# Placing one accumulator at the right end of SBUF and one constant among the experts' tiles, so that every large tile begins at a multiple of 512 bytes

## The chip, the cores and the metric

One Trainium2 chip, one of its cores. The metric is the device time of one launch in microseconds (us), lower being better. The kernel before takes 572.62 us, the median of three runs (572.4 to 574.07).

## What is computed

Three stages in float32, the output of one being the input of the next: causal linear attention with a decay per head, a dense layer pair with a squared ReLU, and a layer pair with eight experts, of which each token uses one.

```python
# attention: q, k, v are (2, 8, 768, 64), in blocks of 64
intra = (qb @ kb.T * Dmask) @ vb
inter = (qb * lam_pow) @ kv_state
kv_state = lam_block * kv_state + (kb * rev_pow).T @ vb
x = out.transpose(0, 2, 1, 3).reshape(1536, 512)
# dense layer pair: w_in is (512, 2048), w_out (2048, 512)
h = np.maximum(x @ w_in, 0.0)
x = h * h @ w_out
# experts: w1 is (8, 512, 1024), w2 (8, 1024, 512)
e_idx = np.argmax(x @ w_gate, axis=1)
out[mask] = gate_w * eom * (np.maximum(x[mask] @ w1[e], 0.0) @ w2[e])
```

## The kernel before

Products that need more than one pass of rounding are made of three: each operand is split into a rounded high part and a remainder (names ending in h and l), and high times high, high times low and low times high are added up in PSUM. A split is a copy on ScalarE (ACT) that writes the high part and a subtraction on VectorE (DVE) or GpSimd (POOL) that writes the low part.

**Attention** runs over 12 units (batch, 128 rows). SP loads q, k and v four units ahead, in order, mixed with raw pieces `st` of w_in and w_out. TensorE (PE) transposes q and k (L257, L259), makes the scores (L287), the output (L301, L305) and the state (L331).

**The dense pair** goes over three chunks of 512 tokens (`ch`) and, in each, over 16 blocks of 128 hidden columns (`f`): 48 steps `s`. In step s, PE makes the hidden block with 12 matmuls of 512 columns (`mm1`, L360; weights `wih`, `wil`; moving data `xTh`, `xTl`) and adds the block of two steps earlier to four output accumulators with 12 more (`mm2`, L488; weights `woh`, `wol`; moving data `gh`, `gl`). Between them `act1` makes gh and gl: ACT the ReLU `r` (L367) and, in the first chunk, the square `g` (L370), then gh (L377); DVE gl (L378). In the first chunk ACT and DVE also turn the loaded weights from 64-bit to 32-bit floats (L130 on ACT; L131, L134 and L138 on DVE, two pieces a step), and the order of both engines' work is that of the text. Between the blocks of chunks 1 and 2 stand the routing of the chunk before (L519 to L701), some 20 short PE jobs.

**The experts**: `emm1` (L925) makes eight hidden blocks with 12 matmuls each, 192, 256 or 384 tokens wide by the expert's count, `emm2` (L947) the output of up to three groups of 128 tokens, 24 matmuls of 512 columns a group. The weights of w1 (L801, L802) are split into the space that xTh and xTl leave. Groups j = 1 and 2 stand behind a branch, with nothing else for PE between their matmuls.

**Where tiles lie.** SBUF is handed out by pools as stacks, from the left end up or, with `side="right"`, from the right end down. `const` (small tables, the accumulator `sacc` of 480 bytes and the constant `over` of 32 among them) comes first on the left, then xTh and xTl, the raw weight buffers `w1`, `w2` of even experts, and the stage's pools. The right side holds q and k during attention (pool ldqk), and after it the split weights wih, wil, woh and wol (pool sp); the first gathered rows `xg0` reuse wih and wil. The experts' own pools (ep, xe, ec) come after the dense pair's are given back; ec holds the raw weights of odd experts.

In a matmul, `lhsT` is what PE loads as weights (LDWEIGHTS, shown as PEld) and `rhs` what it streams:

```python
nc.tensor.matmul(out=ps, lhsT=w_[:, kk, :], rhs=x_[:, kk, tk], ...)          # L360: wih, wil | xTh, xTl
nc.tensor.matmul(out=acc[ch][cb], lhsT=w_[:, cs], rhs=x_, ...)               # L488: woh, wol | gh, gl
nc.tensor.matmul(out=ea[j], lhsT=h_[:, f, js], rhs=w_, ...)                  # L947: hh, hl | w2h, w2l
```

Every such weight block is 128 floats, 512 bytes of each partition, and follows the one before it without a gap.

Of the kernel before, what the change touches and what calls it, by code (L numbers as in the profile page):

```python
# [9 lines left out]
F32 = mybir.dt.float32  # L10
# [14 lines left out]
def attn_moe_kernel(ctx, tc, q, k, v, lam, w_in, w_out, w_gate, w_ogate, w1, w2, out):  # L25
# [4 lines left out]
    E, _, F2 = w1.shape  # L30
    P = 128
# [9 lines left out]
    NG = NSL + 1  # L41
    NW = 5

    ctx.enter_context(tc.manual_schedule())
    const = ctx.enter_context(tc.tile_pool(name="const", bufs=1))
# [20 lines left out]
    wg = const.tile([P, KC, 32], F32, name="wg")  # L66
    nc.gpsimd.memset(wg, 0.0)
    cnti = const.tile([P, E], I32, name="cnti")
    over = const.tile([P, E], F32, name="over")
    overi = const.tile([P, 1], I32, name="overi")  # L70
    caps = const.tile([P, E], F32, name="caps")
    nc.gpsimd.memset(caps, float(NG * P))
# [3 lines left out]
    nc.gpsimd.memset(csum, 0.0)  # L76
    sidx = const.tile([P, NG, E], I32, name="sidx")
    gidx = const.tile([P, NG, E], I32, name="gidx")
    sacc = const.tile([P, NG, NW, E], F32, name="sacc")
    gate = const.tile([P, NG, E], F32, name="gate")  # L80
    pp1 = const.tile([P, 1], F32, name="pp1")
    nc.gpsimd.iota(pp1, [[0, 1]], base=1, channel_multiplier=1, allow_small_or_imprecise_dtypes=True)
# [539 lines left out]
    def route_poh(ch, j):  # L622
        pos, pay = rps[ch]
        poh = (xe[0] or gp[0]).tile([P, NTT, P], BF16, tag="poh", name="poh", bufs=3 if xe[0] else 2)
        for t in range(NTT):
            nc.vector.tensor_scalar(out=poh[:, t, :], in0=slots[:, j * P:(j + 1) * P], scalar1=pos[:, t, :],
                                    scalar2=None, op0=ALU.is_equal)
        rhs_[ch, j] = poh
# [45 lines left out]
    def route_slot(ch, j):  # L674
        slot_mm(ch, [j])
        slot_fin(ch, [j])
# [105 lines left out]
    def w2_of(e, f):  # L782
        return w2r[(e * NF2 + f) // (NF2 // 2)][:, f % (NF2 // 2), :]

    side = {1: [route_base, route_logits], 2: [route_max], 3: [route_rank, route_sum, route_pay], 4: [route_gate, route_gate1, route_gate2],
            5: [lambda c: route_poh(c, 0)], 6: [lambda c: route_slot(c, 0), lambda c: route_poh(c, 1)],
            7: [lambda c: route_slot(c, 1), lambda c: route_poh(c, 2)], 8: [lambda c: route_slot(c, 2)]}
# [75 lines left out]
    ep = ctx.enter_context(tc.tile_pool(name="ep", bufs=1, reuse_waits="tile"))  # L863
# [13 lines left out]
    xg = [ep.tile([P, DM], F32, tag=f"xg{j}", name="xg") for j in range(NG)]  # L877
    ys = [ep.tile([P, DM], F32, tag=f"y{j}", name="y") for j in range(NG)]

    tt = ep.tile([P, 2], I32, name="tt")  # L880
    ti = ep.tile([P, 1], I32, name="ti")

    def gather(out_, ix):
# [212 lines left out]
```

## Time and profile before

| | |
|---|---|
| time, median of 3 runs | 572.62 us |
| profiled execution, its own time | 572.36 us |
| its span | 570.6 us |
| PE busy in the span | 549.9 us (96%) |
| DVE / ACT / POOL busy | 361.4 (63%) / 304.3 (53%) / 148.5 (26%) |
| clock granted to PE | 1.00 in every slice but the last |

The span is one execution seen by the hardware profiler. The stages lie at about 0 to 68 us (attention), 63 to 344 us (the dense pair) and 344 to 562 us (experts). "Busy" of PE counts a matmul from its start to the modelled end of its last column, and neighbours overlap: the time that a matmul costs a stream of matmuls is the distance between two starts, not its duration. Rows that name several forms average over them.

### The profile page before, as it was taken

What the parts mean: (1) busy time and instruction counts of PE and PEld (TensorE: products, weight loads), DVE (VectorE), ACT (ScalarE), POOL (GpSimd) and SP (SyncE); (2) the same over time, 40 slices, a digit from 0 to 9 for tenths busy, and PEclk for the clock granted to TensorE, in tenths of its full rate; (3) what the DMA queues carried; (4) which work ended last, traced back from release to release, by engine and by line L of the source; (5) the groups of instructions that cost most, each with busy time, mean ns of one, the idle gap of its engine ahead of it and who ended that gap; (6) DMA issues with size and microseconds to landing.
All of it is one profiled execution on the core that took longest, in us unless ns stands there. A gap on an engine that the chain in (4) does not pass through costs nothing. (4 is left out here: it accounts for less than half of the span.)

```text
span 570.6 us, 9451 instructions
## 1 busy us (share of the span) xinstructions
PE 549.9 (96%) x3418; PEld 461.9 (81%) x3418; DVE 361.4 (63%) x728; ACT 304.3 (53%) x580; POOL 148.5 (26%) x149
## 2 busy tenths in 40 slices
PE   8998899999999999999999999899999999999994
PEld 7787788888877877887877888789887988888893
DVE  5679988898455664547676446948264839776510
ACT  4766477776543444445454434536364847885610
POOL 4788000000021222422123240350303042240101
PEclk9999999999999999999999999999999999999998
DMA  9999345459000010000000003999638567740000
GB/s 190 234 266 247 124 143 213 167 202 344 25 0 2 20 37 20 0 1 0 20 20 19 20 0 134 382 250 302 199 121 277 183 212 243 262 153 21 10 22 24
DMA packets 75044, 72.87 MB, mean 128 GB/s; under 512 B 30181, under 2 KB 61029, under 8 KB 74976
## 3 DMA queue, kind: packets, MB, share of 16 engines
q1 hardware_dynamic: 70624, 62.96, 36.4%
q0 software_dynamic: 4064, 8.91, 5.0%
q8 instruction: 42, 0.69, 0.5%
q14 instruction: 26, 0.21, 0.1%
q10 hardware_dynamic: 288, 0.10, 0.1%
HBM read 65.84 MB, written 9.29 MB: 132 GB/s over the span
## 5 line engine op out<-in xcount | busy, mean ns | idle before, releaser
L348 POOL TENSOR_TENSOR wol<-woF,woh 128x512 fp32r<-128x512 f32 x32 | 41.6, 1300 | 228.1 <-ACT woh L347 228.1
L378 DVE TENSOR_TENSOR gl<-g,gh 128x512 fp32r<-128x512 f32 x48 | 52.9, 1103 | 67.8 <-ACT gh L377 67.8
L925 PE MATMUL ph<-xh,xTh 128*128 128x192 f32 (+2 forms) x256 | 77.4, 303 | 6.4 <-PEq L1060 2.7
L940 DVE SCALAR_TENSOR_TENSOR hl<-ph,hh 128x384 fp32r<-128x384 f32 (+1 forms) x64 | 34.5, 539 | 68.2 <-ACT hh L939 68.2
L360 PE MATMUL ps<-xTh,wih 128*128 128x512 f32 x192 | 77.5, 404 | 0.0
L488 PE MATMUL acc<-gh,woh 128*128 128x512 f32 x192 | 76.1, 396 | 0.3 <-DVE x1T L500 0.2
L488 PE MATMUL acc<-gl,woh 128*128 128x512 f32 x192 | 75.8, 395 | 0.0
L360 PE MATMUL ps<-xTl,wih 128*128 128x512 f32 x192 | 75.8, 395 | 0.0
L360 PE MATMUL ps<-xTh,wil 128*128 128x512 f32 x192 | 75.8, 395 | 0.0
L488 PE MATMUL acc<-gh,wol 128*128 128x512 f32 x192 | 75.8, 395 | 0.0
L925 PE MATMUL ph<-xh,xTl 128*128 128x192 f32 (+2 forms) x256 | 74.6, 292 | 0.0
L925 PE MATMUL ph<-xl,xTh 128*128 128x192 f32 (+2 forms) x256 | 74.3, 292 | 0.0
L347 ACT CAST woh<-woF 128x512 fp32r<-128x512 f32 x48 | 29.6, 616 | 60.3 <-PE acc L488 60.2
L925 PEld LDWEIGHTS ph<-xh,xTh 128*128 128x128 f32 x256 | 48.6, 190 | 15.0 <-DVE hl L940 7.3
L939 ACT ACTIVATE hh<-ph 128x384 fp32r<-128x384 f32 (+1 forms) x64 | 30.7, 480 | 41.0 <-PE ph L925 37.9
L367 ACT ACTIVATE r<-ps 128x512 f32<-128x512 f32 x48 | 28.6, 595 | 39.1 <-PE ps L360 39.1
L925 PEld LDWEIGHTS ph<-xl,xTh 128*128 128x128 f32 x256 | 48.6, 190 | 0.7
L925 PEld LDWEIGHTS ph<-xh,xTl 128*128 128x128 f32 x256 | 48.8, 191 | 0.0
L884 POOL DMA_INDIRECT xg<-x1d,gidx x21 | 23.4, 1116 | 88.9 <-PE pt L904 66.0
L802 DVE TENSOR_TENSOR xTl<-w1r,xTh 128x512 fp32r<-128x512 f32 x64 | 44.1, 690 | 0.1
L488 PEld LDWEIGHTS acc<-gh,woh 128*128 128x128 f32 x192 | 36.0, 187 | 9.9 <-DVE x1T L500 1.2
L952 POOL DMA_INDIRECT out_dram<-y,sidx x23 | 23.6, 1027 | 76.4 <-ACT y L951 67.9
(185 smaller groups left out, 1160.1 us busy)
## 6 DMA issues: line engine op xcount, KB each, us to landing
w1r<-in_moe_w_dram SPq DMA_DIRECT2D x32, 512.0 KB, 6.5
w2r<-in_moe_w_dram SPq DMA_DIRECT2D x32, 512.0 KB, 7.1
st<-in_moe_w_in_dram SPq DMA_DIRECT2D x16, 512.0 KB, 3.8
st<-in_moe_w_out_dram SPq DMA_DIRECT2D x16, 512.0 KB, 4.4
q<-in_q_dram SPq DMA_DIRECT2D x24, 128.0 KB, 4.4
k<-in_k_dram SPq DMA_DIRECT2D x12, 256.0 KB, 4.6
v<-in_v_dram SPq DMA_DIRECT2D x12, 256.0 KB, 5.0
x1d<-xr SPq DMA_DIRECT2D x12, 256.0 KB, 2.0
```

What stands on the lines that cost most here:

```text
L347: nc.scalar.copy(out=hi, in_=src)
L348: eng.tensor_tensor(out=lo, in0=src, in1=hi.bitcast(F32), op=ALU.subtract)
L360: nc.tensor.matmul(out=ps, lhsT=w_[:, kk, :], rhs=x_[:, kk, tk], start=n == 0, stop=n == 3 * KC - 1)
L367: nc.scalar.activation(out=r, in_=ps, func=AF.Relu)
L378: nc.vector.tensor_tensor(out=gl, in0=g, in1=gh.bitcast(F32), op=ALU.subtract)
L488: nc.tensor.matmul(out=acc[ch][cb], lhsT=w_[:, cs], rhs=x_, start=f == 0 and i == 0, stop=f == NF - 1 and i == 2)
L802: eng.tensor_tensor(out=lo, in0=src, in1=hi.bitcast(F32), op=ALU.subtract)
L884: nc.gpsimd.indirect_dma_start(out=out_, out_offset=None, in_=x1d[:, :], in_offset=bass.IndirectOffsetOnAxis(ap=ix, axis=0), bounds_check= ...
L925: nc.tensor.matmul(out=ps[:, 0:N], lhsT=w_[:, kk, :], rhs=x_[:, kk, 0:N], start=n == 0, stop=n == 3 * KC - 1)
L939: nc.scalar.activation(out=hh[:, f, ts_], in_=ps[:, ts_], func=AF.Relu)
L940: nc.vector.scalar_tensor_tensor(out=hl[:, f, ts_], in0=ps[:, ts_], scalar=0.0, in1=hh[:, f, ts_].bitcast(F32), op0=ALU.max, op1=ALU.subtract)
L952: nc.gpsimd.indirect_dma_start(out=outs[j][:, :], out_offset=bass.IndirectOffsetOnAxis(ap=sidx[:, j, e:e + 1], axis=0), in_=ys[j], in_offs ...
```

## The change

The accumulator `sacc` leaves `const` for a pool of its own at the right end. The constant `over` leaves `const` for the experts' pool ep, and a pad of 224 bytes is put there behind the small tile `tt`. Nothing else is edited.

```diff
@@ -66,7 +66,6 @@
     cnti = const.tile([P, E], I32, name="cnti")
-    over = const.tile([P, E], F32, name="over")
     overi = const.tile([P, 1], I32, name="overi")
@@ -76,7 +75,9 @@
     gidx = const.tile([P, NG, E], I32, name="gidx")
-    sacc = const.tile([P, NG, NW, E], F32, name="sacc")
+
+    rend = ctx.enter_context(tc.tile_pool(name="rend", bufs=1, side="right"))
+    sacc = rend.tile([P, NG, NW, E], F32, name="sacc")
     gate = const.tile([P, NG, E], F32, name="gate")
@@ -877,7 +878,9 @@
+    over = ep.tile([P, E], F32, name="over")
     tt = ep.tile([P, 2], I32, name="tt")
+    ep.tile([P, 56], F32, name="pad")
     ti = ep.tile([P, 1], I32, name="ti")
```

The instructions of both programs, their order on each of the five engines and the semaphores that they wait for are the same, row for row. What differs are the addresses. Byte offsets in a partition (the first buffer of each name), and what is left of them when divided by 512:

| tiles | before | mod 512 | after | mod 512 |
|---|---|---|---|---|
| xTh, xTl | 21504, 46080 | 0 | 20992, 45568 | 0 |
| raw w1, w2 of even experts | 70656, 87040 | 0 | 70144, 86528 | 0 |
| hh, hl, w2h, w2l, xh, xl, xg, y | 136192 (hh) | 0 | 135680 (hh) | 0 |
| st, r, g, gh, gl, v, kd, sm, qd | 189440 (gh) | 0 | 188928 (gh) | 0 |
| raw w1, w2 of odd experts | 177920, 194304 | 256 | 177664, 194048 | 0 |
| q, wih, wil (right side) | 212960 (wih) | 480 | 212480 (wih) | 0 |
| k, woh, wol (right side) | 221152 (woh) | 480 | 220672 (woh) | 0 |
| sacc | 19808 | 352 | 228864 | 0 |
| over | 18976 | 32 | 172544 | 0 |

So the two groups whose place within 512 bytes changes and that are large are the right side (480 to 0) and the odd experts' raw weights (256 to 0). Everything on the left moves down by 512 bytes together. Small tiles (sidx, gidx, lgT, poh and others) move too, by 32 to 512 bytes.

## Rows read from the trace of the kernel before

**Rows 1.** Busy us, dense pair: PE, PEld, DVE, ACT, POOL; PEclk, DMA share, GB/s

```profile
75.00:340.00 265.00, 264.72 (x1250) 211.08 (x1249) 168.63 (x333) 135.31 (x243) 51.49 (x40) 1.00 0.18 64
```

**Rows 2.** Groups by form, two of the matmuls (busy us, mean ns, idle before)

```profile
L360 PE MATMUL ps<-xTh,wil 128*128 128x512 f32 x192 | 75.8, 395 | 0.0
...
L947 PE MATMUL ea<-xTl,hh 128*128 128x512 f32 x102 | 40.0, 392 | 0.0
```

**Rows 3.** Timeline of PE, dense pair, first matmuls of blocks (start, us, what)

```profile
94.27 0.40 PE L360 MATMUL ps<-xTh,wih 128*128 128x512 f32 x1
...
97.07 0.40 PE L488 MATMUL acc<-gh,woh 128*128 128x512 f32 x1
...
99.87 0.40 PE L360 MATMUL ps<-xTh,wih 128*128 128x512 f32 x1
```

**Rows 4.** Timeline of PE, experts 0 and 1, groups of L947

```profile
376.15 0.48 PE L947 MATMUL ea<-xTh,hh 128*128 128x512 f32 x1
...
378.30 0.39 PE L947 MATMUL ea<-xTh,hh 128*128 128x512 f32 x1
...
381.70 0.33 PE L925 MATMUL ph<-xh,xTh 128*128 128x384 f32 x1
...
405.37 0.39 PE L947 MATMUL ea<-w2h,hh 128*128 128x512 f32 x1
...
410.81 0.39 PE L947 MATMUL ea<-w2h,hh 128*128 128x512 f32 x1
```

**Rows 5.** Timeline of PE, dense pair, a block behind a routing job

```profile
273.92 0.48 PE L360 MATMUL ps<-xTh,wih 128*128 128x512 f32 x1
...
276.79 0.40 PE L488 MATMUL acc<-gh,woh 128*128 128x512 f32 x1
```

**Rows 6.** Timelines of DVE and PE while DVE rests

```profile
342.66 0.69 DVE L500 COPY x1T<-acc 128x512 f32<-128x512 f32 x1 [1.75 <-PE acc L488]
...
341.06 0.40 PE L488 MATMUL acc<-gh,woh 128*128 128x512 f32 x1
...
342.46 0.40 PE L488 MATMUL acc<-gh,woh 128*128 128x512 f32 x1
```

**Rows 7.** Groups by form, weight loads of L360 and of two transposes

```profile
L360 PEld LDWEIGHTS ps<-xTh,wil 128*128 128x128 f32 x192 | 36.0, 188 | 8.9
...
L904 PEld LDWEIGHTS pt<-ident,xg 128*128 128x128 f32 x56 | 6.9, 140 | 1.8
...
L259 PEld LDWEIGHTS psk<-ident,k 128*128 128x128 f32 x48 | 5.5, 141 | 0.8 <-DMA k<-in_k_dram 0.6 <-ACT ca L268 0.2
```

**Rows 8.** Timeline of PE, expert 6: three matmuls of L947 between L925

```profile
494.56 0.42 PE L947 MATMUL ea<-xTh,hh 128*128 128x512 f32 x1
...
495.28 0.25 PE L925 MATMUL ph<-xh,xTh 128*128 128x192 f32 x1
```

**Rows 9.** Timelines of DVE (steps 1 and 11) and PE (step 1), first chunk

```profile
78.81 0.69 DVE L378 TENSOR_TENSOR gl<-g,gh 128x512 fp32r<-128x512 f32 x1
...
134.54 0.69 DVE L378 TENSOR_TENSOR gl<-g,gh 128x512 fp32r<-128x512 f32 x1
...
80.51 0.39 PE L488 MATMUL acc<-gl,woh 128*128 128x512 f32 x1
```

**Rows 10.** Waits of weight loads, 150 to 344 us (us in total, times, longest)

```profile
PEld acc L488 <- DVE x1T L500: 1.2, 2, 0.6
```

**Rows 11.** DMA issues (count, size, median us to landing)

```profile
k<-in_k_dram SPq DMA_DIRECT2D x12, 256.0 KB, 4.6
v<-in_v_dram SPq DMA_DIRECT2D x12, 256.0 KB, 5.0
```

**Rows 12.** Splits on ACT by form, and the reads of raw w1 (min/median/max ns)

```profile
L377 ACT CAST gh<-g 128x512 fp32r<-128x512 f32 x48 | 29.6, 617 | 5.4 <-DVE g L372 5.4
L347 ACT CAST woh<-woF 128x512 fp32r<-128x512 f32 x48 | 29.6, 616 | 60.3 <-PE acc L488 60.2
...
L801 ACT CAST xTh<-w1r x64: 607/612/632, 258.0 to 539.1; 128x512 fp32r<-128x512 f32 x64
```

## The prediction

> **What bounds the kernel now.** First I read the busy time by stretches. From 75 to 340 us, the dense pair, PE is busy 264.72 of 265 us at a granted clock of 1.00, DVE 168.63, ACT 135.31, and the DMA share is 0.18 [rows 1]. So this half of the span is as long as PE's matmuls take, and nothing but the distance from one matmul's start to the next can shorten it. Durations don't tell that distance: they are 395 ns for a dense matmul and 392 for an expert one, both 512 columns wide [rows 2]. The timeline does. In the dense pair the first matmuls of three blocks stand at 94.27, 97.07 and 99.87 us: 12 matmuls in 2.80 us, 233.3 ns each, in mm1 and mm2 alike [rows 3]. In the experts, 24 matmuls of the same width follow each other from 405.37 to 410.81 us: 5.44 us, 226.7 ns each [rows 4]. At the 2.4 GHz of a granted 1.00 these are 560 and 544 cycles. The same instruction costs 6.7 ns more in the dense pair, and there are 48 x 24 = 1152 of them: up to 7.7 us.
>
> What makes the difference? Not other engines: before 342.66 us DVE has rested for 1.75 us, and inside that rest six matmuls take from 341.06 to 342.46, 233 ns each [rows 6]. Not the moving tensor or the PSUM bank: mm1 (xTh, one bank for 12) and mm2 (gh and gl, a new bank after every three) run at the same 2.80 [rows 3]. Not a passing disturbance either: after the restart at 376.15 an expert group is at its pace by 378.30 (from there 15 matmuls in 3.40 us, to 381.70 [rows 4]), while the dense blocks never reach it. What mm1 and mm2 share and L947 hasn't is the place of the weights: wih to wol begin 480 bytes past a multiple of 512, hh and hl at a multiple. That is inference from one kernel; no row shows an off-place tile moved.
>
> **The change, part by part.** It removes and adds no instruction, and moves none. It changes places.
>
> *Right side, weights of mm1 and mm2 (480 to 0).* If the place is the cause, a step of 24 matmuls goes from 5.60 to 5.44 us, 0.16 less. Three things take some of 48 x 0.16 = 7.7 back.
> First, the first chunk has a second clock. DVE's gl of step 1 starts at 78.81, that of step 11 at 134.54: 5.573 us a step [rows 9]. In the text's order DVE waits for ACT's woh and ACT's g for DVE's last gl; the two pace each other, slightly faster than PE's 5.600, so they don't follow PE now and won't speed up with it. At step 1 gl ends at 78.81 + 0.69 = 79.50 and is used at 80.51 [rows 9]: 1.01 us to spare. Ten steps on it is 10 x 0.027 more, 1.28. PE gains 0.16 a step until that slack is used, about step 7, and then runs at 5.573, some 0.13 us of waiting a step. By step 12, the last with conversions ahead of its gl, it is ahead by the slack there, 1.2 with some semaphore time off, not 13 x 0.16 = 2.1. The other 35 steps bring 5.6. Together 6.8.
> Second, restarts. A dense block behind a routing job takes 273.92 to 276.79 = 2.87 us, 0.07 over 2.80 [rows 5]; an expert group behind transposes takes 376.15 to 381.70 = 5.55, 0.11 over 5.44 [rows 4]. In chunks 1 and 2 there are 16 such jobs: 16 x 0.04 = 0.6.
> Third, mm2 of a new chunk waits for the old accumulators to be copied out (two waits, 1.2 us of weight loads [rows 10]); one mm1 block hides part of that and becomes 0.08 shorter: 2 x 0.08 = 0.2.
> The sum is 6.8 - 0.6 - 0.2 = 6.0 us less. What is late next is gl in steps 7 to 12, and nothing after. Its bounds are 0, if the place is not the cause, and 7.7.
>
> *Writers and the other readers of these tiles.* ACT writes woh (off place) in 616 ns and gh (in place) in 617 [rows 12], so the splits keep their times: 0.
> The weight loads of transposes last 141 ns from k (off place) and 140 from xg (in place) [rows 7]: attention's PE work keeps its time.
>
> *q and k as targets of transfers (480 to 0).* k lands 4.6 us after its issue, v, as large and already in place, 5.0 [rows 11]: no penalty to remove. The only wait for it is 0.6 us of weight loading at the first k [rows 7], so the bounds are -0.6 and, by the 0.4 between k and v, +0.4; I take 0, nearest to the equal rows of ACT.
> The Trainium skill ("DMA: Bandwidth & Descriptors", How a descriptor splits into AXI transactions) says that a descriptor which doesn't start at a multiple of 256 bytes costs extra beats, which would speak for faster loads of q and k. The landings of k and v do not show it, and by it the sum would be at most the 0.6 us of that wait better.
>
> *Raw weights of odd experts (256 to 0).* Half of ACT's 64 reads of w1 are from these; all 64 lie between 607 and 632 ns [rows 12]: 0, hidden besides by an expert's PE work.
>
> *sacc, over, the pad.* A few DVE operations of 8 to 120 elements read or write them; by the equal rows of ACT a place costs nothing: 0. The experts' matmuls keep their places within 512 bytes and their distances to each other: 0.
>
> **The rivals.** *A: the place is not the cause.* Then the dense step stays at 5.60 and the time at 572.4, with at most 0.6 for the loads. For it: the weight load itself lasts 188 ns in the dense pair [rows 7], short against a 233 ns step, and the transposes' loads don't care. The weights of mm1 and mm2 also share that they lie at the far right end of SBUF, which the change leaves so. Against it: the dense pair's pace is constant, and wherever weights in place run long enough the pace is the lower one. So the loss must come from how loading and streaming meet, which a load's own duration needn't show.
> The Trainium skill ("TensorE: Matmul & The Clock Gate", Step-by-step: what each phase is for) says that the two read ports of PE are independent and that loading the next weights doesn't take read bandwidth from the running matmul. By that rule no place of the weights changes the pace, and the time is A's. The two paces of one instruction speak against it, but don't refute it.
>
> *B: part of the gain.* The pace settles between the two, or in one of mm1 and mm2 only: half of the 5.6 us behind step 12, and 0.16 x 13 / 2 = 1.0 before it, less the 0.8 for restarts and evacuations halved: 3.4 less, 569.0.
>
> *C: in place, the two streams meet badly.* Weights in place can be slow too: behind 192-wide matmuls three of L947 take 494.56 to 495.28 = 0.72 us, 240 ns each [rows 8]. If mm1 and mm2, which alternate every 12, locked into that, it would cost 1152 x (240 - 233.3) = 7.7 us: 580.1, slower. It decides from a pace above 233.3 + 1.7 / 1.152 = 234.8 ns on. Against it: that pace follows a change of width, and mm1 and mm2 have one width; with one width the groups in place settled within eight matmuls, at 226.7 [rows 4].
>
> **How the numbers follow.** The profiled execution is 572.36 us: a span of 570.6 and 1.8 around it, 0.26 under the median of 572.62. Less 6.0 it is 566.4; against the median 566.6; I predict 566.5. The forecast has a chance of 0.56, B 0.12, A 0.25, C 0.07. About 0.3%, 1.7 us, is what a measurement of this kernel can tell from no change. So faster is 0.56 + 0.12 = 0.68, within 0.3% 0.25, slower 0.07. The forecast's own range is 565.0 (the whole 7.7 us) to 568.0. Forecast and B hold only 0.68, so the range must reach A's 572.4 and its spread: 565.0 to 572.9, which leaves C out.
>
> **What would show it.** Right: in the profile after, blocks of mm1 and mm2 in chunks 1 and 2 begin 2.72 us apart where no routing job stands between, not 2.80; PE waits for DVE's gl by 0.1 us or so in each of steps 7 to 12, a wait that isn't there now; the first routing matmul behind the dense pair starts some 6 us earlier than its 344 us; expert groups stay at 5.44; ACT, DVE and LDWEIGHTS durations stay. Wrong: blocks 2.80 apart and a time near 572 mean A, blocks between 2.72 and 2.80 mean B, above 2.80 C. If blocks are at 2.72 but the time falls by far less than 6, the cap in the first chunk is tighter than the slack I read, or the experts start later than their weights allow.

## The result and the profile after

The changed kernel takes 566.45 us (median of 4 runs, 566.28 to 566.57), the kernel before, run beside it, 572.89 (4 runs, 572.4 to 574.07). The ratio is 0.9885, with a 95% interval of 0.9873 to 0.9897: 1.15% faster, where 566.5 us was forecast. The profiled execution took 566.57 us with a span of 564.8, against 572.36 and 570.6.

In the dense pair, the answer to [rows 1] first. Columns: stretch, its length, busy us of PE, PEld, DVE, ACT and POOL with their instructions, granted clock, DMA share, GB/s.

```profile
75.00:340.00 265.00, 264.53 (x1301) 215.00 (x1301) 170.74 (x337) 136.38 (x245) 54.69 (x44) 1.00 0.19 65
```

PE is as busy as before and at the same clock, but puts 1301 matmuls into these 265 us, not 1250: of those with 512 columns 1115, not 1100, and 36 short ones of the last routing, which now falls inside the stretch. The timeline of PE shows why; first the three blocks that answer [rows 3], then three blocks of the first chunk that follow DVE's gl (start, us, what).

```profile
93.65 0.39 PE L361 MATMUL ps<-xTh,wih 128*128 128x512 f32 x1
96.36 0.39 PE L489 MATMUL acc<-gh,woh 128*128 128x512 f32 x1
99.08 0.39 PE L361 MATMUL ps<-xTh,wih 128*128 128x512 f32 x1
...
112.81 0.39 PE L489 MATMUL acc<-gh,woh 128*128 128x512 f32 x1
115.66 0.39 PE L361 MATMUL ps<-xTh,wih 128*128 128x512 f32 x1
118.38 0.39 PE L489 MATMUL acc<-gh,woh 128*128 128x512 f32 x1
```

The first two blocks take 2.71 and 2.72 us, not 2.80: 226.7 ns a matmul. From 112.81 on a block of mm2 takes 2.85 and one of mm1 2.72, 5.57 together: PE has caught up with the loop of DVE and ACT. The profile names that new wait in the row of mm2's weight loads (busy us, mean ns, idle before and what ended it), while the load itself still lasts 188 ns, as in [rows 7]:

```profile
L489 PEld LDWEIGHTS acc<-gl,woh 128*128 128x128 f32 x192 | 36.0, 188 | 9.1 <-DVE gl L379 1.8
```

Where the dense pair ends, and where the experts begin, on PE's timeline of the kernel after and then of the kernel before:

```profile
338.30 1.28 PE L520 MATMUL pl<-x1T,wg 128*32 128x128 f32 x32
348.55 0.39 PE L928 MATMUL ph<-xh,xTh 128*128 128x256 f32 x1 [0.46 <-DVE xl L913]
```

```profile
343.95 1.28 PE L519 MATMUL pl<-x1T,wg 128*32 128x128 f32 x32
354.19 0.39 PE L925 MATMUL ph<-xh,xTh 128*128 128x256 f32 x1 [0.45 <-DVE xl L910]
```

The routing behind the last block starts 5.65 us earlier and the experts 5.64. That is nearly all of the 5.8 us by which the span is shorter. The time went where it was looked for, into the pace of the dense matmuls.

### The profile page after: what moved, and what is told of

Read it like the earlier page. It is cut to its first block, busy times and chain, and to the rows that moved or that the text cites. A ratio compares the mean times of both kernels' runs of the same rounds, so it can differ in the third digit from the quotient of the medians.

```text
span 564.8 us, 9451 instructions
## 1 busy us (share of the span) xinstructions
PE 544.3 (96%) x3418; PEld 462.3 (82%) x3418; DVE 360.8 (64%) x728; ACT 304.1 (54%) x580; POOL 148.3 (26%) x149
## 4 chain that ended last, share of the span: by engine, by line
PE 55%; issue 28%; POOL 6%; DVE 4%; DMA 3%; ACT 1%; POOLq 1%; SPq 0%; another core or an unknown queue 0%; ACTq 0%
PE acc L489 23%; PE ps L361 22%; POOL out_dram L955 3%; POOL xg L887 2%; PE po L302 2%; PE po L306 2%; PE ps L288 2%; DMA xg<-x1d,gidx 2%; DMA w1r<-in_moe_w_dram 1%; PE px L702 1%; PE psq L258 1%; ACT ca L264 1%; DMA out_dram<-y,sidx 1%; PE pw__157 L205 1%; DVE xTl L310 1%
## 5 line engine op out<-in xcount | busy, mean ns | idle before, releaser
L489 PEld LDWEIGHTS acc<-gl,woh 128*128 128x128 f32 x192 | 36.0, 188 | 9.1 <-DVE gl L379 1.8
```

The costliest lines, as they stand in the source:

```text
L489: nc.tensor.matmul(out=acc[ch][cb], lhsT=w_[:, cs], rhs=x_, start=f == 0 and i == 0, stop=f == NF - 1 and i == 2)
```

## The experiments

The theory on record was that weights off a multiple of 512 bytes slow the matmuls that use them. Four kernels test it by parts, four more move the other operand and look for the size of the step, one returns q and k alone, one tries another distance for the experts' weights, and two test the cap in the first chunk.

**Back off place, the weights alone.** The changed kernel with 32 bytes behind the split weights, so that wih, wil, woh and wol are at 480 again and all else stays.

```diff
     def split_out(s):
         splits[s] = split(woF[:, s % NF, :], "wo", ...)
+        if s == 0:
+            sp[0].tile([P, 8], F32, name="spad", bufs=1)
```

> The changed kernel with one pad of 32 bytes behind the split weights: wih, wil, woh and wol begin 480 bytes past a multiple of 512 again, all else (q, k, the odd experts' raw weights, sacc) stays where the change put it. Theory P (the place of the weights sets the pace of the dense pair): blocks of mm1 and mm2 are 2.80 us apart again, and the time is 572.4 to 572.9, that of the kernel before. Rival T (the gain is from the loads of q and k, or from any other moved tile): blocks stay at 2.72 us and the time at 566.5.

Measured: 571.97 us (10 runs, 571.67 to 572.4), ratio to the kernel before 0.998 (0.997 to 0.9991). PE's timeline:

```profile
93.91 0.40 PE L361 MATMUL ps<-xTh,wih 128*128 128x512 f32 x1
96.71 0.40 PE L491 MATMUL acc<-gh,woh 128*128 128x512 f32 x1
99.51 0.40 PE L361 MATMUL ps<-xTh,wih 128*128 128x512 f32 x1
```

2.80 again. From the first dense matmul (62.92) to the routing behind the last block (343.62) this kernel takes 280.70 us, the kernel before 280.68 and the changed one 274.99: these four tiles are the whole gain of the dense pair. The median is 0.9 us under the kernel before's (0.5 to 1.7 by the interval), and under the 572.4 to 572.9 expected; that difference doesn't come from this stretch. With the pad ahead of that split in the code, not behind it, only mm1's weights are at 480.

> The changed kernel with a pad of 32 bytes between the split weights: wih and wil (mm1) at 480, woh and wol (mm2) in place. Theory P, with each matmul paid for by itself: blocks of mm1 take 2.80 us, those of mm2 2.72 (in the first chunk, where mm2 waits for gl, no more than 5.60 for both); the time lies half-way, about 569.5. Rival S (a disturbed phase carries over from one block to the next, since mm1 and mm2 alternate): both near 2.80, about 572.4; or, if the good phase carries over, both near 2.72, 566.5.

Measured: 568.18 us (3 runs), ratio 0.9916 (0.989 to 0.9942), nearly three quarters of the gain kept.

```profile
93.46 0.39 PE L361 MATMUL ps<-xTh,wih 128*128 128x512 f32 x1
96.26 0.39 PE L491 MATMUL acc<-gh,woh 128*128 128x512 f32 x1
98.98 0.39 PE L361 MATMUL ps<-xTh,wih 128*128 128x512 f32 x1
```

A block of mm1 takes 2.80 and one of mm2 2.72: each pays for its own weights. More is kept than the half that was expected (277.10 us for the same stretch, 63% of the 5.69): a step of 2.80 + 2.72 = 5.52 us gains only 0.05 on the 5.57 of the loop of DVE and ACT, so that the slack of 1.01 [rows 9] lasts and no block of mm2 waits for gl in the first chunk.

**The odd experts' raw weights alone.** The kernel before with a pad of 256 bytes that brings only these to a multiple of 512.

```diff
+    ep.tile([P, 64], F32, name="pad")
```

> The kernel before with a pad of 256 bytes among the experts' tiles, so that the raw weights of odd experts alone come to a multiple of 512. Theory P: these are read by ACT and DVE and written by DMA, nothing of it sets an end; 572.4 to 572.9, blocks of the dense pair at 2.80 us. Rival T: some of the gain, 1 to 6 us, shows here.

Measured: 572.96 us (10 runs), ratio 0.9995 (0.9981 to 1.0009), dense blocks 2.80. This part of the change does nothing that can be measured.

**The experts' weights off place.** The changed kernel with hh and hl at 480.

```diff
+    ep.tile([P, 120], F32, name="hpad")
     hh = ep.tile([P, NF2, NX], F32R, name="hh")
     hl = ep.tile([P, NF2, NX], F32R, name="hl")
+    ep.tile([P, 8], F32, name="hpad2")
```

> The changed kernel with pads around hh and hl, the weights of the second expert matmul (L950 here, L947 before): they begin at 480, all other tiles keep their place within 512 bytes. Theory P: the groups of 24 matmuls of 512 columns that stand alone take 5.60 us instead of 5.44, and the dense pair stays at 2.72 us a block. Some ten such groups, and the interleaved ones change little: 1 to 2 us more than the changed kernel, 567.5 to 568.5. Rival L (the far right end of SBUF is slow at some offsets, places further left are not): groups stay at 5.44, 566.5.

Measured: 568.08 us (2 runs), ratio 0.9908 (0.9873 to 0.9943). One group in the experts has 54 matmuls in a row; its first one and the first matmul behind it, in the changed kernel and then in this one:

```profile
398.25 0.48 PE L950 MATMUL ea<-xTh,hh 128*128 128x512 f32 x1
...
410.61 0.28 PE L928 MATMUL ph<-xh,xTh 128*128 128x256 f32 x1
```

```profile
398.43 0.48 PE L952 MATMUL ea<-xTh,hh 128*128 128x512 f32 x1
...
411.11 0.28 PE L930 MATMUL ph<-xh,xTh 128*128 128x256 f32 x1
```

12.36 us become 12.68, 54 x 6 ns. Weights moved off a multiple of 512 cost the experts about as much per matmul as the change gave back in the dense pair. So far the paces agreed with the theory, and it was still wrong: in all these kernels the moving tiles stood at a multiple of 512.

**Three other places.** Pads put wih and wil at 384, woh and wol at 448, hh and hl at 256.

```diff
+        if s == 0:
+            sp[0].tile([P, 16], F32, name="spad", bufs=1)
         splits[s] = split(woF[:, s % NF, :], "wo", ...)
+        if s == 0:
+            sp[0].tile([P, 16], F32, name="spad2", bufs=1)
...
+    ep.tile([P, 64], F32, name="hpad")
     hh, hl = ...
+    ep.tile([P, 64], F32, name="hpad2")
```

> The changed kernel with pads that put three pairs of weights at three other places past a multiple of 512 bytes: wih and wil (mm1) at 384, woh and wol (mm2) at 448, hh and hl (the experts' second matmuls) at 256; the moving tiles and everything else keep their places. Each theory says which place is bad. If a multiple of 64 is all that weights need (480 is none), blocks of 12 stay at 2.72 us in mm1 and mm2 and expert groups of 24 at 5.44, time 566.5. If it is 128, mm2 alone is slow (2.80), time about 566.5 + 576 x 6.6 ns - what the first chunk's cap hides = 568.2 to 570. If it is 256, mm1 and mm2 are slow, 572. If it is 512, the solo expert groups are slow as well (24 in 5.60), 572 to 573.5. My guess, because the rows of 512 bytes that 128 columns of fp32 fill are what each matmul loads: 64 with 0.5, 512 with 0.3, the others 0.1 each.

Measured: 569.84 us (1 run).

```profile
93.87 0.39 PE L361 MATMUL ps<-xTh,wih 128*128 128x512 f32 x1
96.67 0.39 PE L493 MATMUL acc<-gh,woh 128*128 128x512 f32 x1
99.42 0.39 PE L361 MATMUL ps<-xTh,wih 128*128 128x512 f32 x1
...
401.47 0.48 PE L956 MATMUL ea<-xTh,hh 128*128 128x512 f32 x1
...
413.83 0.28 PE L934 MATMUL ph<-xh,xTh 128*128 128x256 f32 x1
```

384 is slow (2.80; 2.79 as the mean of 29 blocks), 256 is as good as 0 (12.36), and 448 lies between (2.75). No multiple fits: 384 has more powers of two in it than 448 and is worse. My guess of 64 was wrong.

**The moving tiles off place.** A pad of 32 bytes in front of the left side: the dense pair's moving tiles at 32 and its weights at 0, the experts' moving tiles and weights both at 32.

```diff
+    const.tile([P, 8], F32, name="lpad")
```

> The changed kernel with a pad of 32 bytes in front of the left side: the dense pair's moving tiles (xTh, xTl, gh, gl) lie at 32 past a multiple of 512, its weights at 0; of the experts' second matmuls the moving tiles and the weights both lie at 32. If the weights' own place sets the pace, the dense blocks stay at 2.72 us and the expert groups of 24 go from 5.44 to 5.60: time about 568.1, as when the experts' weights alone were moved. If it is the place of either operand, both become slow: 572 to 573.5, or slower if two such prices add. If it is the distance from the weights to the moving tile, the dense blocks become 2.80 and the expert groups stay 5.44: 572. The first theory has 0.7, the second 0.1, the third 0.2.

Measured: 572.8 us (1 run).

```profile
94.51 0.40 PE L362 MATMUL ps<-xTh,wih 128*128 128x512 f32 x1
97.31 0.40 PE L490 MATMUL acc<-gh,woh 128*128 128x512 f32 x1
100.11 0.40 PE L362 MATMUL ps<-xTh,wih 128*128 128x512 f32 x1
...
404.42 0.48 PE L951 MATMUL ea<-xTh,hh 128*128 128x512 f32 x1
...
416.77 0.28 PE L929 MATMUL ph<-xh,xTh 128*128 128x256 f32 x1
```

Here the theory falls. The dense weights lie at a multiple of 512 and run at 2.80; the experts' weights lie at 32 and run at 12.35, the good pace. What decides is how far the weights lie from the moving tile. With the right side 32 bytes lower as well (weights 480, moving 32), the distance is 448:

```diff
+    rend.tile([P, 8], F32, name="rpad")
+    const.tile([P, 8], F32, name="lpad")
```

> As the run before it, and the right side 32 bytes lower as well: in the dense pair the moving tiles lie at 32 and the weights at 480 past a multiple of 512 (a distance that is a multiple of 64), in the experts both at 32. If the weights' own place sets the pace, dense blocks 2.80 us and expert groups 5.60: 572 to 573.5. If the distance from weights to moving tile does it, 2.72 and 5.44: 566.5.

```profile
93.34 0.40 PE L363 MATMUL ps<-xTh,wih 128*128 128x512 f32 x1
96.08 0.40 PE L491 MATMUL acc<-gh,woh 128*128 128x512 f32 x1
98.83 0.40 PE L363 MATMUL ps<-xTh,wih 128*128 128x512 f32 x1
```

Blocks of 2.75 us, as at 448 in the run of three places, and 12.36 for the 54 matmuls in the experts (404.85 to 417.21). I had expected 2.72 of this distance, before 448 was measured; neither theory had 2.75, but the weights' own place (480) would be 2.80. Its time, 573.17 us (1 run), isn't shorter for another reason: its first dense matmul starts at 68.29, 5 us late. In the first 62 us, where q, k and v are loaded, the windows of the kernel before, the changed kernel and this one read:

```profile
0.00:62.00 62.00, 56.40 (x703) 50.03 (x704) 47.05 (x93) 37.76 (x83) 41.69 (x57) 1.00 0.99 224
```

```profile
0.00:62.00 62.00, 56.77 (x703) 50.67 (x704) 47.00 (x93) 37.70 (x83) 41.70 (x57) 1.00 0.87 224
```

```profile
0.00:62.00 62.00, 52.98 (x643) 45.61 (x644) 43.24 (x85) 35.80 (x79) 40.78 (x56) 1.00 1.05 215
```

With q and k in place the DMA engines are busy 0.87 of this stretch, with q and k at 480 for 0.99, at the same 224 GB/s. In this run, with v at 32 as well, the figure is 1.05 (it adds up the times of packets, and can pass 1), at 215 GB/s, and PE gets less done; with v at 32 and q and k in place (the run ahead of this one) it was 0.89 at 224. That is one execution; what made it late is not settled.

**q and k alone.** The changed kernel with q and k at 480.

```diff
+        ldqk.tile([P, 8], F32, name="qpad", bufs=1)
```

> The changed kernel with q and k alone put back to 480 past a multiple of 512, the place that they had; all weights stay at a multiple. If the weights are the whole of the gain, the time is the changed kernel's, 566.5 (566.2 to 566.9), with dense blocks at 2.72. If part of the gain came by the loads of q and k, it is slower by up to the 0.6 us of the one wait for k: 567.1.

Measured: 567.35 us (4 runs, 566.65 to 568.99), ratio to the kernel before 0.9892 (0.987 to 0.9915), beside the changed kernel's 0.9885. Dense blocks are 2.72, the first dense matmul starts at 63.51 (63.31 in the changed kernel), and the DMA share of the first 62 us is 0.99 again: 0.99 in all three traces with q and k at 480, 0.87 to 0.89 in ten of the eleven with them in place, 1.05 in the run above. The intervals overlap: a busier DMA, and no end that it moves for certain. The 0.9 us of the first run above (weights back, q and k in place) may come from here. The three executions with q and k at 480 start their dense pair at 63.27 to 63.51, those with q and k in place anywhere from 62.70 to 64.35 and once at 68.29, so that can't be told.

**More distances.** mm1's weights at 352, mm2's at 416, hh and hl at 64 (pads as above, of 64 and 96 bytes on the right and 64 and 448 on the left).

> The changed kernel with pads as in the sweep before, at three more distances between the weights and the moving tile (moving tiles at a multiple of 512): mm1's weights at 352, mm2's at 416, the experts' hh and hl at 64. So far the distance (weights less moving, modulo 512) set the pace: 0 and 256 gave 226.7 ns a matmul, 448 229, 384 232.6, 480 233.3. If the distance is what counts, mm1 and mm2 are both above 229 (blocks 2.75 to 2.80 us), and the experts at 64 stand off 226.7 too: 229 to 233 (24 in 5.50 to 5.60). If it was the weights' own place that counted, as I first held, and 256 or 64 is merely what it asks for, the experts at 64 run at 226.7 (5.44). Time 570 to 572.

Measured: 574.93 us (1 run).

```profile
93.88 0.40 PE L361 MATMUL ps<-xTh,wih 128*128 128x512 f32 x1
96.69 0.40 PE L493 MATMUL acc<-gh,woh 128*128 128x512 f32 x1
99.49 0.40 PE L361 MATMUL ps<-xTh,wih 128*128 128x512 f32 x1
...
405.25 0.48 PE L956 MATMUL ea<-xTh,hh 128*128 128x512 f32 x1
...
417.94 0.28 PE L934 MATMUL ph<-xh,xTh 128*128 128x256 f32 x1
```

352 takes 2.81, 416 takes 2.80, 64 takes 12.69: all slow. The time lies above the 570 to 572 expected. From the first dense matmul to the routing this execution takes 281.00 us, 6.01 more than the changed kernel's, and from the first matmul of the experts to the end 2.8 more, of which 1.04 is one wait of PE (at 392.02) for a weight split on ACT. And hh and hl at 128, alone (pads of 128 and 384 bytes around them):

> The changed kernel with hh and hl alone moved to 128 past a multiple of 512, the experts' moving tiles and the dense pair as they are. If distances repeat every 256 bytes, 128 is the same as the 384 that mm1 had in the first sweep: 232.6 ns a matmul, 24 in 5.58 us, time about 568. If small distances count by their size, 128 lies between 0 and 256, both good, and can be at 226.7 or anywhere up to 233.3; time 566.5 to 568.1. A pace under 226.7 would be a better place than the change found; I give that 0.1.

Measured: 567.77 us (1 run).

```profile
398.31 0.48 PE L952 MATMUL ea<-xTh,hh 128*128 128x512 f32 x1
...
410.93 0.28 PE L930 MATMUL ph<-xh,xTh 128*128 128x256 f32 x1
```

12.62 us. 128 costs as much as 384 did. All distances (weights less moving, modulo 512) together, with the pace of a matmul from the blocks or groups above. Rows of the dense pair are blocks / 12, read to 0.01 us and so good to about 1 ns. A group has a restart in it, so its row is 226.7 ns [rows 4] and the excess over 12.36 us spread over 54:

| distance | where | measured | ns a matmul |
|---|---|---|---|
| 0 | dense; experts, also with both at 32 | 2.72; 12.36, 12.35 | 226.7 |
| 64 | experts | 12.69 | 232.8 |
| 128 | experts | 12.62 | 231.5 |
| 256 | experts | 12.36 | 226.7 |
| 352 | dense | 2.81 | 234.2 |
| 384 | dense | 2.79 (mean of 29) | 232.5 |
| 416 | dense | 2.80 | 233.3 |
| 448 | dense, twice (0 and 448; 32 and 480) | 2.75; 2.74 and 2.75 | 229.2 |
| 480 | dense, twice (0 and 480; 32 and 0); experts | 2.80; 12.68 | 233.3; 232.6 |

Only 0 and 256 are at the good pace, and nothing is better. A period of 256 bytes fits all rows (0 beside 256 and 128 beside 384 are the pairs that test it); what happens at a multiple of 256 in the hardware, the runs don't show. The dense pair at 256 was not tried, nor were distances under 32.

**The cap in the first chunk.** DVE's share of the weight splits there (wol) moved to GpSimd, which does it in the other chunks:

```diff
-        ... "wo", [P, DM], nc.vector if s < NF else nc.gpsimd)
+        ... "wo", [P, DM], nc.gpsimd)
```

> The changed kernel with one thing more: in the first chunk the split of wol (0.69 us a step) goes to GpSimd, as in the other two chunks, and no longer to DVE. My reading of the first chunk is that DVE and ACT pace each other at 5.573 us a step there and that PE, now at 5.44, has to wait for gl from step 7 on by about 0.13 us a step. Then the loop falls under 5.44, PE's waits for gl go, mm2 blocks of the first chunk are 2.72 throughout, and the time falls by 6 or 7 x 0.13 = 0.8 to 0.9: 565.6, under both kernels. If the cap is something else, or if GpSimd's 1.29 us instead of 0.69 makes mm2 wait for wol, the time stays at 566.5 or rises by up to 1.

Measured: 573.07 us (11 runs), ratio to the kernel before 1.0004 (0.9995 to 1.0013): the whole gain gone, far above both 565.6 and the rise of at most 1 us that was expected otherwise. DVE and GpSimd in one step:

```profile
111.28 1.37 DVE L349 TENSOR_TENSOR wil<-wiF,wih 128x512 fp32r<-128x512 f32 x1 [1.11 <-ACT wih L348]
```

```profile
110.80 1.29 POOL L349 TENSOR_TENSOR wol<-woF,woh 128x512 fp32r<-128x512 f32 x1 [4.87 <-ACT woh L348]
```

wil lasts 1.37 us, not 0.69: it starts while GpSimd's subtraction runs, and ends 0.56 us behind that one's end at 112.09, so most of a usual 0.69 lies behind it. And DVE now waits for wih, which ACT makes behind woh, so the loop is 6.17 us (wil at 111.28 and 117.45), longer than before. The Trainium skill ("SBUF — State Buffer", Who interferes with whom) says that a DVE instruction with two SBUF inputs contends with a GpSimd instruction that reads SBUF; both are subtractions of two SBUF tiles, and the trace agrees. The kernel before had shown it already, in the chunks where wol is on GpSimd: gl, 0.69 us in the first chunk [rows 9], lasts 1.38 there beside a wol.

```profile
228.63 1.38 DVE L378 TENSOR_TENSOR gl<-g,gh 128x512 fp32r<-128x512 f32 x1 [2.42 <-ACT gh L377]
```

```profile
228.16 1.30 POOL L348 TENSOR_TENSOR wol<-woF,woh 128x512 fp32r<-128x512 f32 x1 [4.72 <-ACT woh L347]
```

The loop itself, in the changed kernel, DVE and then ACT (what ended an idle time, in brackets):

```profile
112.29 0.69 DVE L379 TENSOR_TENSOR gl<-g,gh 128x512 fp32r<-128x512 f32 x1
...
114.25 0.69 DVE L349 TENSOR_TENSOR wol<-woF,woh 128x512 fp32r<-128x512 f32 x1 [0.59 <-ACT woh L348]
...
117.87 0.68 DVE L379 TENSOR_TENSOR gl<-g,gh 128x512 fp32r<-128x512 f32 x1
```

```profile
113.07 0.64 ACT L371 ACTIVATE g<-r 128x512 f32<-128x512 f32 x1 [0.56 <-DVE gl L379]
113.61 0.60 ACT L348 CAST woh<-woF 128x512 fp32r<-128x512 f32 x1
```

gl releases g (one buffer), g stands ahead of woh on ACT, woh releases DVE's wol, and six operations on stands the next gl: 5.58 us. Nothing makes woh wait for g but ACT's order. So ACT's splits of a step go ahead of g:

```diff
         g = gp[0].tile([P, NTC], F32, tag="g", name="g", bufs=1)
+        if mid is not None and 1 <= s < NF:
+            mid()
+            mid = None
         if s < NF:
```

> The changed kernel with one more edit, in the order of ACT in steps 1 to 11 of the first chunk: the splits woh and wih of the step come before the squaring g, not behind it; DVE's order and everything else stay. In the trace of the changed kernel the loop of DVE and ACT there runs from gl (112.29) by g, which waits for gl (113.07), and woh (113.61) to DVE's wol (114.25), where DVE has waited 0.59 us, and six more DVE operations back to gl (117.87): 5.58 us. If that loop is what caps the first chunk, woh no longer waits for gl, DVE's 0.59 goes, its own work of a step is 5.0 us, less than PE's 5.44, and every block of mm2 in the first chunk is 2.72, not up to 2.89: seven blocks give back 0.9 us together, time 565.6 (565.2 to 566.1). If the cap were GpSimd-free contention, the loads of st or the bank of PSUM instead, the blocks stay above 2.8 and the time stays at 566.5.

Measured: 565.85 us (4 runs, 565.29 to 566.84), ratio to the kernel before 0.9876 (0.986 to 0.9893).

```profile
111.01 0.39 PE L361 MATMUL ps<-xTh,wih 128*128 128x512 f32 x1
113.73 0.39 PE L492 MATMUL acc<-gh,woh 128*128 128x512 f32 x1
116.45 0.39 PE L361 MATMUL ps<-xTh,wih 128*128 128x512 f32 x1
```

```profile
116.42 0.62 ACT L348 CAST woh<-woF 128x512 fp32r<-128x512 f32 x1 [0.84 <-PE acc L492]
```

From the fourth on, every block of the first chunk is 2.72, and woh now waits for PE to leave its buffer: PE sets the pace. From the first dense matmul to the first of the experts this execution takes 284.21 us (64.35 to 348.56), the changed kernel's 285.24 (63.31 to 348.55), 1.03 less. The median is 0.6 us under the changed kernel's, with intervals that overlap; the blocks show the step, the time alone doesn't prove it.

## Why the prediction was right, and where it wasn't

*The pace.* Right in size: 2.72 us a block, 226.7 ns a matmul, where nothing else waits, while weight loads stay at 188 ns and ACT's splits at 615 to 617. The clue was right too: two paces of one instruction at one granted clock. That no other engine makes the difference was concluded from too little: [rows 6] show DVE at rest only, and in the same stretch ACT starts a copy (341.96) and GpSimd a memset (342.08). The experiments settle it: with the same instructions in the same order, moving tiles alone changes the pace.

*The cause.* Named too simply. The step that failed is "what mm1 and mm2 share and L947 hasn't is the place of the weights". They share the distance between weights and moving tile as well; as the moving tiles were at a multiple of 512 in all the rows, place and distance were one number there, and the text ruled the moving tensor out only by comparing two kinds that lay at the same place. With moving tiles at 32, weights in place were slow (2.80) and weights at 32 were fast (12.35). That the forecast came out all the same was luck in this respect: the moving tiles lie at a multiple of 512 before and after, so the change sets the place and the distance right together. By the theory on record one would also have put the moving tiles at 32 and the weights at 0 without worry, and lost some 6 us (572.8, 1 run).

The Trainium skill ("TensorE: Matmul & The Clock Gate", Step-by-step: what each phase is for) was weighed as the case for no gain: that loading weights doesn't take read bandwidth from the running matmul. The runs disagree with what was drawn from it, that no place of the weights changes the pace: with the same instructions in the same order, the distance between the two tiles alone moves it from 226.7 to 233.3 ns. Whether read bandwidth is what gets lost, they don't show.

*The first chunk.* Right, in mechanism and place: mm2 waits for gl in the blocks from 107.26 to 140.72, seven of them (2.82 to 2.90 us; steps 6 to 12, where 7 to 12 were named), and the next block of mm1 stands at 143.57, in the kernel before at 144.67: 1.14 us ahead when each is counted from its first dense matmul (63.31 and 63.27), where 1.2 was forecast. That this was the loop of DVE and ACT is shown by the last experiment, which opens it.

*The rest of the sum.* From the first dense matmul to the routing behind the last block, the changed kernel needs 5.69 us less (5.65 by the rows above, and 0.04 for the start), where 6.0 was forecast. 1.14 of it is there by 143.57. Behind that stand 33 blocks of mm1 and 35 of mm2, 68 x 0.08 = 5.44, of which 5.69 - 1.14 = 4.55 came: restarts and evacuations cost 0.89, not 0.8. The two blocks that wait for the accumulators, 3.17 and 3.23 us before and 3.26 and 3.27 after, take 0.29 of it, where 0.2 was forecast; 0.60 is left for the restarts, as forecast. The forecast had counted 70 blocks there, two too many, 0.16. With the 0.06 of the first chunk these make up the 0.3. That the median lies within 0.1 us of the forecast is luck in part: the two profiled executions differ by 5.79 us, the medians of four runs each by 6.44. One restart to look at, in the changed kernel, beside [rows 5]:

```profile
269.85 0.48 PE L361 MATMUL ps<-xTh,wih 128*128 128x512 f32 x1
272.66 0.39 PE L489 MATMUL acc<-gh,woh 128*128 128x512 f32 x1
```

2.81 us, 0.09 over 2.72; before it was 0.07 over 2.80.

*What was put at nothing.* The odd experts' raw weights: nothing, by the run with them alone. q and k: nothing that the time shows, though the DMA share of the first 62 us falls from 0.99 to 0.87 at the same GB/s. Near-equal landings [rows 11] had not let me see that. The Trainium skill ("DMA: Bandwidth & Descriptors", How a descriptor splits into AXI transactions) had said that a descriptor that doesn't start at a multiple of 256 bytes costs extra beats, though it tells this of the bytes that are fetched, not of the place written to. The share agrees, as 480 is no such multiple; the time shows no gain from it.

*The rivals.* A (place is not the cause) and B (half) fall by the blocks of 2.72. A was right that the weights' place alone is not the cause, and wrong in the time that followed from it. C (two streams meet badly) doesn't occur between mm1 and mm2.

## What to carry to other kernels

When one instruction runs at two paces at the same clock and nothing waits, compare the addresses of all its operands, and with each other, not only with a round number. In this kernel, weights and moving tile a multiple of 256 bytes apart run at 226.7 ns a matmul, the other distances tried at 229 to 234; a few bytes of constants at the other end of SBUF can decide it, and one run with the other operand moved tells a place from a distance. When the bound engine gets faster, look for a loop just beneath it: here reordering three operations on ACT opened it, and moving a subtraction to GpSimd, beside which DVE's took 1.37 us, made it longer.

## What was not expected of the hardware

- The pace of TensorE goes by the distance in bytes from the weights' tile to the moving tile (modulo 512): 226.7 ns a matmul at 0 and 256, 229.2 at 448, 231.5 to 234.2 at 64, 128, 352, 384, 416 and 480.
- Where a transfer lands changes how long the DMA engines are busy with it: with q and k at 480 bytes past a multiple of 512 a share of 0.99 of the first 62 us, at a multiple 0.87, both at 224 GB/s.
- A DVE subtraction of two SBUF tiles takes 1.37 us, not 0.69, when it starts while one on GpSimd (1.29) runs.
